# Starting the first feed-forward step's products inside the attention visits, with constant products on TensorE before them

## The chip, the cores and the metric

The kernel runs on one core of one Trainium2 chip. The metric is the device time of one execution in microseconds (us). Before the change the median of three runs is 909.93 us, from 908.02 to 910.37. Five engines work side by side and wait for each other through semaphores: TensorE (PE in the profile; its weight loads are listed as PEld), VectorE (DVE), ScalarE (ACT), GpSimd (POOL) and SyncE (SP), which here only issues DMAs. Each engine takes its instructions in the order in which the program issues them.

## What is computed

An attention over short windows, whose result is the input of a feed-forward layer. All arrays are float32; a product that needs more than the fast format of TensorE gives is made of three products of high and low parts.

```python
# attention: batch 8, heads 8, sequence 576, head_dim 64
scores = q @ k.T / 8          # masked: heads 0-3 see the last 32 keys,
attn = softmax(scores)        # heads 4-7 every 4th of the last 128 keys
x = (attn @ v) as rows of 512 # one row per token: 4608 tokens
# feed-forward: 512 -> 2048 -> 512
h = x @ w_in
g = h * erf(softplus(h))
out = g @ w_out
```

## The kernel before

**The attention in units.** The 32 head pairs (8 batches times 4 pairs) are numbered `it`; each has 9 blocks of 64 queries, and a unit is four such blocks, so there are 72 units (`NU`). A unit `n` goes through: `scores` (32 small matmuls, L214, into an `sp` bank), `mask_max` (four DVE operations, L225), `exponents` (four ACT activations, L235), `normalize` (a DVE reciprocal, L247, and a POOL product, L248), and, three units later (`LAG` = 3), `transposes` (two matmuls, L253), `turned` (a copy of the result, L257), `values` (32 small matmuls, L272), `rows` (ACT copies, L314) and `finish`, which splits a finished head pair into a high part (ACT, L319) and a low part (DVE, `part_lo`, L325). For batch 0 these parts lie in `xs[0]` to `xs[3]`, one per head pair.

**The visits.** Units 0 to 13 (`FIRST` = 14) are handled before any feed-forward work, one `first_visit(n)` each (L349 to L373): the later half of unit m = n - 3 and the early half of unit n, in a written order. On TensorE the order in a visit is transposes(m), scores(n), values(m). With nine blocks per pair and four per unit, the pairs 0, 1, 2 and 3 of batch 0 end with units 2, 4, 6 and 8, so their high parts are made in visits 5, 7, 9 and 11, and their low parts in visits 6, 8, 10 and 11. In visits 1 to 9 (`EARLY`) ACT and DVE also turn weights, which arrive as 64-bit floats, into high and low float32 parts (`prep_act`: L427, L432; `prep_dve`: L441, L445, L446, L447), and the end of each such piece lets SP load the next one (L412). The copy `turned` is ACT's in those visits, DVE's afterwards. The four pieces of `w_in` that the first two steps need come first.

**What SP does in a visit.** `load_qk(n + 2)` (L198) overwrites the buffer that scores(n) has read, so it waits for them; `load_v(n - 1)` (L202) waits for values(n - 3). SP takes its DMAs in order, so whatever stands behind such a wait starts later too.

**The steps.** The feed-forward work is cut into chunks of 512 tokens and, within these, steps of two 128-wide tiles of the 2048 features. A step `t` has two halves j = 0, 1; the main loop runs over x = 2t + j. In each half `mm1(t, j)` (L499) makes h for one tile: for each of the four 128-wide slices `cc` of the model dimension (which is a head pair) three products 128x512, twelve in all, L509, into the one PSUM bank `h`. `take` (L648, L651) copies the bank to `hc` on DVE and so frees it. In the first two steps the order in a half is: turn (transposes and the copy) of a unit, weight pieces, `mm1`, `take`, exponents, then values and scores of the next units. After both halves ACT makes softplus (L655) and erf (L658), each with a table load, DVE makes the product and its parts (`gate`: L665, L668, L669), and two steps later `mm2` (L671, L683) multiplies with `w_out` into the four `acc` banks.

**PSUM.** There are eight banks: `sp0`, `sp1`, `tx` (named `bank` in the code), `acc0` to `acc3` and `h`. During the visits, `tx` and `h` are not used; `tx` is first used by `mm1_fast`, from the fourth chunk on (L624). `plain`, an SBUF tile, is first used when the sums of weight blocks are built (`sum_whole`, L515).

Of the kernel before, what the change touches and what calls it, by code (L numbers as in the profile page):

```python
# [12 lines left out]
BF16 = mybir.dt.bfloat16  # L13
# [5 lines left out]
P = 128  # L19
# [12 lines left out]
CC = DM // P  # L32
FT = DF // P
TOK = 512
# [31 lines left out]
FREE = FIRST - LAG + 4  # L66

EARLY = 9

SAVED = 2 * (HALF + 1) + 1  # L70

# [55 lines left out]
def key_start(u, s):  # L127

    return s * STRIP + (WIN if (SPU * u) // NSTRIP != (SPU * u + s) // NSTRIP else 0)
# [7 lines left out]
def attn_moe_kernel(ctx: ExitStack, tc: tile.TileContext, qk, v, masks, eye, w_in, w_out, out):  # L137
    nc = tc.nc
# [16 lines left out]
    win_at = win.rearrange("p (a j k i c n) -> p a j k i c n", a=SPC, j=PAIR, k=2, i=2, c=2)  # L155
# [12 lines left out]
    plain = one.tile([P, 2 * TOK], F32, name="plain")  # L168
# [3 lines left out]
    bank = ps.tile([P, TOK], F32, name="tx")  # L172
# [5 lines left out]
    def place(u, p):  # L178


        if u < FREE:
            return acc[(u + 1 + 2 * p) % 4][:, p * P:(p + 1) * P]
        at = PARTS * P + (u in second) * P
        return spb[p][:, at:at + P]
# [6 lines left out]
    xs = [one.tile([P, 2, S], F32R, name=f"x{cc}") for cc in range(CC)]  # L191
# [3 lines left out]
    def load_qk(u):  # L195
        if u < NU:
            n = QW + key_start(u, SPU - 1) + KEYS
            nc.sync.dma_start(out=qkz[u % 2][:, 0:n], in_=qk[u, :, 0:n])  # L198
# [9 lines left out]
    def scores(u):  # L208
        i = u % 2
        for s in range(SPU):  # L210
            at, (p, r) = QW + key_start(u, s), divmod(s, SIDE)
            for h in range(2):
                hs = slice(h * D, (h + 1) * D)
                nc.tensor.matmul(sps[h][r * STRIP:(r + 1) * STRIP, i, p, :], qkz[i][hs, s * STRIP:(s + 1) * STRIP],  # L214
                                 qkz[i][hs, at:at + KEYS], start=True, stop=True,
                                 tile_position=(h * D, r * STRIP))

    def mask_max(u):

        pr = probs[u] = work.tile([P, 2 * PARTS, KEYS], F32, name="prob", bufs=LAG + 1)  # L220
        nmax = maxes[u] = small.tile([P, 2 * PARTS], F32, name="nmax", bufs=LAG + 1)
        for h in range(2):
            for p in range(PARTS):
                g = PARTS * h + p
                nc.vector.tensor_tensor_reduce(  # L225
                    out=pr[:, g, :], in0=sps[h][:, u % 2, p, :], in1=mask[QUADS.index(kinds(u, p))],
                    scale=-SCALE, scalar=BIG,
                    op0=ALU.add, op1=ALU.min, accum_out=nmax[:, g:g + 1],
                )
# [12 lines left out]
    def normalize(u):  # L242
        rinv = small.tile([P, 2 * PARTS], F32, name="rinv")

        if u >= FIRST:
            nc.vector.tensor_scalar(sums[u], sums[u], 1.0e-9, None, op0=ALU.add)  # L246
        nc.vector.reciprocal(out=rinv, in_=sums.pop(u))  # L247
        nc.gpsimd.tensor_tensor(probs[u], probs[u], rinv.broadcast_to([P, 2 * PARTS, KEYS]), op=ALU.mult)  # L248

    def transposes(u):  # L250
        pr = probs.pop(u)
        for h in range(2):
            nc.tensor.transpose(out=turn_place(u)[:, h * P:(h + 1) * P],  # L253
                                in_=pr[:, PARTS * h:PARTS * (h + 1), :].rearrange("p a k -> p (a k)"), identity=ident)

    def turned(u, copy):
        copy(out=pz[u in second][:, 0:2 * P], in_=turn_place(u))  # L257
# [7 lines left out]
    def values(u):  # L265
        vt, pt = vz[u % 2], pz[u in second]
        for s in range(SIDE):
            qs = slice(s * STRIP, (s + 1) * STRIP)
            for p in range(PARTS):
                ks, xp = slice(p * KEYS, (p + 1) * KEYS), place(u, p)  # L270
                for h in range(2):
                    nc.tensor.matmul(xp[h * D:(h + 1) * D, qs], vt[ks, s, h, :],  # L272
                                     pt[ks, h * P + s * STRIP:h * P + (s + 1) * STRIP], start=True, stop=True,
                                     tile_position=(p * KEYS, h * D))
# [37 lines left out]
    def rows(u):  # L312
        for to, src in rows_of(u):
            nc.scalar.copy(out=to, in_=src)  # L314
# [7 lines left out]
    def part_lo():  # L322
        while halved:
            hi, lo, src = halved.pop(0)
            nc.vector.tensor_tensor(out=lo, in0=src, in1=hi.bitcast(F32), op=ALU.subtract)  # L325
# [20 lines left out]
    def has(u):  # L346
        return 0 <= u < NU

    def first_visit(n):  # L349

        m = n - LAG
        copy = nc.scalar.copy if 1 <= n <= EARLY else nc.vector.tensor_copy
        if has(m):
            transposes(m)
        scores(n)
        load_qk(n + 2)
        if has(m):
            turned(m, copy)
        if 1 <= n <= EARLY:
            prep_act()  # L360
        if has(m):
            values(m)
        if has(n - 2):
            normalize(n - 2)
        mask_max(n)
        part_lo()
        if has(m):
            rows(m)
            finish(m)
        if m == NBLK - 1:  # L370
            part_lo()
        exponents(n)
        load_v(n - 1)  # L373
# [47 lines left out]
    def prep_act():  # L421


        calls[0] += 1
        if made:
            w, hi, lo = made.popleft()
            nc.scalar.copy(out=hi, in_=like(w, hi))  # L427
            rest.append((calls[0], w, hi, lo))
        if staged:
            i, d, hi, lo = staged.popleft()  # L430
            w = io.tile([P, TOK], F32, name="w", bufs=4)
            nc.scalar.activation(out=w, in_=d[:, :, 1].bitcast(F32), func=AF.Abs, scale=REBASE)  # L432
            begun.append((calls[0], i, d, hi, lo, w))
# [20 lines left out]
    h = ps.tile([P, TOK], F32, name="h")  # L454
# [44 lines left out]
    def mm1(t, j):  # L499
        c, ftp, _ = STEPS[t]  # L500
        hi, lo = at[c]
        ft = ftp * PAIR + j

        ccs = list(range(CC))
        if ends(t) and j == PAIR - 1:
            ccs = ccs[twice:] + ccs[:twice]
        for k, cc in enumerate(ccs):
            for i, (w, x) in enumerate(((0, hi), (0, lo), (1, hi))):
                nc.tensor.matmul(h, win_at[:, ftp, j, cc // 2, w, cc % 2, :], x[cc],  # L509
                                 start=(k == 0 and i == 0), stop=(k == CC - 1 and i == 2))  # L510

    ws = dram.tile([SPC, P, len(LEFT) * KIND], F32, name="ws")
# [133 lines left out]
    hs, ls, gs = {}, {}, {}  # L646

    def take(t, j):  # L648
        if j == 0:
            hs[t], ls[t] = (work.tile([P, PAIR, TOK], F32, name=n) for n in ("hc", "s"))  # L650
        nc.vector.tensor_copy(out=hs[t][:, j], in_=h)  # L651

    def argument(t):

# [68 lines left out]
            (nc.scalar if last and tt % 2 else nc.sync).dma_start(out=out[r:r + P, :], in_=o)  # L723

    with tc.manual_schedule():
        load_qk(0)
        nc.sync.dma_start(out=cst[:, 0:NMASK * KEYS], in_=masks)
        load_qk(1)
        nc.sync.dma_start(out=ident, in_=eye)
        for n in range(FIRST):  # L730
            if n < 3:
                load_w(n)
            first_visit(n)
            if 1 <= n <= EARLY:
                prep_dve()
# [15 lines left out]
        for x in range(2 * (NT + 2)):  # L751
            t, j = divmod(x, 2)
# [161 lines left out]
```

## Time and profile before

| | |
|---|---|
| median of the three runs | 909.93 us |
| the profiled execution | 909.24 us |
| its span, first to last instruction | 907.1 us |
| PE busy | 877.6 us, 9072 matmuls |
| DVE busy | 670.0 us |
| ACT busy | 600.5 us |
| POOL busy | 77.6 us |
| moved by DMA | 188.87 MB, 208 GB/s on average |
| visits (first scores to the transposes of unit 11) | 3.49 to 48.20 us |
| first product of h | 48.54 us |
| first product of `mm2` | 72.93 us |

A row of the timeline gives the start and the length in us, the engine, the line, the operation, the tile written and those read, shapes, and how many such instructions in a row are merged into it; in square brackets how long the engine had been idle before it, and what ended that wait. A row of the windows gives, for a stretch of time, the busy time of each engine, the DMA share and GB/s. A row of the chain of work that ended last gives start, length and what it was.

### The profile page before, as it was taken

To read this page: it belongs to the slowest core of one execution; us is meant where nothing else is said; L and a number is where in the kernel's file an instruction comes from. 1 tells how busy PE (TensorE), PEld (TensorE's weight loads), DVE (VectorE), ACT (ScalarE), POOL (GpSimd) and SP (SyncE) were. 2 spreads that over 40 slices of the span, in tenths; PEclk is the share of its full clock that TensorE was granted. 3 is DMA by queue.
4 is the path that set the end of the run, shared out by engine and by line. 5 is a ranking of instruction groups with operands and counts; after the bars stand their busy time and mean duration, and the time that the engine had idled before them with its cause. 6 is when DMAs were issued, how large, how long until landed. Compare 5 with 4: busy or idle time off the path is not lost.

```text
span 907.1 us, 22745 instructions
## 1 busy us (share of the span) xinstructions
PE 877.6 (97%) x9072; PEld 756.1 (83%) x9072; DVE 670.0 (74%) x1703; ACT 600.5 (66%) x1266; POOL 77.6 (9%) x96
## 2 busy tenths in 40 slices
PE   4699999999999999999999999999999999999998
PEld 3467777888887878888988989888988998998996
DVE  5878878876788888767866777678666866776555
ACT  7879879876678687666776676669654644545442
POOL 2312100000011100000000000001000000000000
PEclk9999999999999999999999999999999999999999
DMA  8874344433459688677668765777567546656521
GB/s 301 282 234 146 124 164 131 154 109 103 159 184 330 214 299 306 234 276 243 212 220 284 253 214 203 279 258 258 176 244 231 179 152 228 236 174 204 199 85 46
DMA packets 69449, 188.87 MB, mean 208 GB/s; under 512 B 9184, under 2 KB 17632, under 8 KB 63200
## 3 DMA queue, kind: packets, MB, share of 16 engines
q1 hardware_dynamic: 69056, 186.91, 60.4%
q8 instruction: 71, 1.16, 0.5%
q10 hardware_dynamic: 288, 0.52, 0.2%
q14 instruction: 34, 0.28, 0.1%
HBM read 153.85 MB, written 33.55 MB: 207 GB/s over the span
## 4 chain that ended last, share of the span: by engine, by line
PE 85%; DVE 7%; ACT 4%; issue 2%; DMA 2%; POOL 1%; SPq 0%; DVEq 0%; POOLq 0%; ACTq 0%
PE acc L683 40%; PE h L630 15%; PE tx L630 12%; PE h L509 11%; PE sp L272 3%; PE sp L214 2%; PE sp L253 1%; DMA dbl<-in_w_in_dram 1%; ACT prob L235 1%; DVE s L665 1%; DVE hc L651 1%; DVE w L446 1%; DVE w L447 1%; DVE ghi L668 1%; DVE win L441 0%
## 5 line engine op out<-in xcount | busy, mean ns | idle before, releaser
L683 PE MATMUL acc<-wout_hi,ghi 128*128 128x512 f32 x576 | 228.4, 396 | 0.2 <-DVE dbl L701 0.2
L683 PE MATMUL acc<-wout_lo,ghi 128*128 128x512 f32 x576 | 225.6, 392 | 0.0
L655 ACT ACTIVATE s<-hc 128x1024 f32<-128x1024 f32 x72 | 76.5, 1063 | 188.4 <-DVE hc L644 171.1
L683 PE MATMUL acc<-wout_hi,glo 128*128 128x512 f32 x576 | 158.9, 389 | 0.0
L683 PEld LDWEIGHTS acc<-wout_hi,glo 128*128 128x128 f32 x576 | 108.1, 188 | 22.7
L683 PEld LDWEIGHTS acc<-wout_hi,ghi 128*128 128x128 f32 x576 | 108.6, 188 | 20.0 <-DVE dbl L701 0.6
L683 PEld LDWEIGHTS acc<-wout_lo,ghi 128*128 128x128 f32 x576 | 108.6, 189 | 19.6
L248 POOL TENSOR_TENSOR prob<-prob,rinv 128x256 f32<-128x256 f32 x72 | 69.3, 972 | 537.6 <-DVE ssum L246 313.6
L669 DVE TENSOR_TENSOR glo<-s,ghi 128x512 fp32r<-128x512 f32 x144 | 100.0, 694 | 5.5 <-PE acc L683 0.5
L235 ACT ACTIVATE prob<-prob,nmax 128x64 f32<-128x64 f32 x288 | 96.4, 338 | 7.1 <-DVE nmax L225 6.7
L509 PE MATMUL h<-x,win 128*128 128x512 f32 x384 | 98.9, 401 | 1.2 <-DVE hc L651 1.2
L665 DVE TENSOR_TENSOR s<-hc,s 128x1024 f32<-128x1024 f32 x72 | 93.3, 1295 | 8.7 <-ACT s L658 8.6
L630 PE MATMUL h<-win 128*128 128x256 f32 x720 | 98.1, 283 | 0.0
L655 ACT ACT_TABLE_LOAD x72 | 92.4, 1283 | 1.3
L658 ACT ACT_TABLE_LOAD x72 | 92.4, 1283 | 1.3
L630 PEld LDWEIGHTS h<-win 128*128 128x128 f32 x720 | 91.6, 192 | 0.0
L509 PEld LDWEIGHTS h<-x,win 128*128 128x128 f32 x384 | 72.9, 192 | 17.8 <-DVE hc L651 2.1
L658 ACT ACTIVATE s<-s 128x1024 f32<-128x1024 f32 x72 | 76.3, 1060 | 0.8
L668 DVE CAST ghi<-s 128x512 fp32r<-128x512 f32 x144 | 68.1, 473 | 3.1 <-PE acc L683 0.6
L225 DVE CUSTOM_DVE_ANT_0 prob<-sp,cst 128x64 f32<-128x64 f32 x288 | 45.3, 219 | 30.2 <-ACT rows L314 20.5
L314 ACT COPY rows<-sp 128x128 f32<-128x128 f32 (+7 forms) x167 | 27.9, 308 | 57.0 <-PE sp L214 54.7
L640 DVE TENSOR_TENSOR hc<-h,hc 128x512 f32<-128x512 f32 x48 | 33.2, 691 | 41.2 <-PE h L630 40.9
(105 smaller groups left out, 1246.4 us busy)
## 6 DMA issues: line engine op xcount, KB each, us to landing
win<-ws SPq DMA_DIRECT2D x48, 1024.0 KB, 6.2
win<-ws SPq DMA_DIRECT2D x48, 768.0 KB, 4.5
v<-in_v_dram SPq DMA_DIRECT2D x72, 256.0 KB, 4.3
qk<-in_qk_dram SPq DMA_DIRECT2D x48, 272.0 KB, 4.1
dbl<-in_w_in_dram SPq DMA_DIRECT2D x16, 512.0 KB, 4.5
dbl<-in_w_out_dram SPq DMA_DIRECT2D x16, 512.0 KB, 3.7
ws<-x SPq DMA_DIRECT2D x32, 256.0 KB, 4.8
qk<-in_qk_dram SPq DMA_DIRECT2D x24, 288.0 KB, 4.2
```

The lines of the kernel that those rows point to most:

```text
L225: nc.vector.tensor_tensor_reduce(out=pr[:, g, :], in0=sps[h][:, u % 2, p, :], in1=mask[QUADS.index(kinds(u, p))], scale=-SCALE, scalar=BIG ...
L235: nc.scalar.activation(out=probs[u][:, j, :], in_=probs[u][:, j, :], func=AF.Exp, scale=-1.0, bias=nmax[:, j:j + 1], accum_out=sums[u][:, ...
L248: nc.gpsimd.tensor_tensor(probs[u], probs[u], rinv.broadcast_to([P, 2 * PARTS, KEYS]), op=ALU.mult)
L509: nc.tensor.matmul(h, win_at[:, ftp, j, cc // 2, w, cc % 2, :], x[cc], start=(k == 0 and i == 0), stop=(k == CC - 1 and i == 2))
L630: nc.tensor.matmul((h, bank)[b][:, half * HN:(half + 1) * HN], w[:, k, wi, c, :], x[:, xi, c, :], start=(c == 0 and n == 0), stop=(c == 1 ...
L640: nc.vector.tensor_tensor(out=a[:, 0:2], in0=x, in1=a[:, 2:3].broadcast_to([P, 2, HN]), op=ALU.add)
L655: nc.scalar.activation(out=ls[t], in_=hs[t], func=AF.Softplus)
L658: nc.scalar.activation(out=ls[t], in_=ls[t], func=AF.Erf)
L665: nc.vector.tensor_tensor(out=e, in0=hc, in1=e, op=ALU.mult)
L668: nc.vector.tensor_copy(out=ghi, in_=e[:, j])
L669: nc.vector.tensor_tensor(out=glo, in0=e[:, j], in1=ghi.bitcast(F32), op=ALU.subtract)
L683: nc.tensor.matmul(acc[tt], g[:, tt * P:(tt + 1) * P], w[:, ft, :], start=(first and w is wout_hi and g is ghi), stop=(last and g is glo))
```

## The change

Three things are added and two follow from them.

1. At the program's start GpSimd fills `idle`, the first 512 bfloat16 elements per partition of `plain`, with ones, and TensorE runs eight products `busy(8)` of these constants, 128x128 by 128x512, into the bank `h`, before anything else. Nothing reads their result.
2. In visits 0 to 6 (`AHEAD` = 7) TensorE gets more of these: six between the scores and the end of the visit in visits 0 to 2, and in visits 3 to 6 two between scores(n) and values(m) and two behind values(m). Together with the first eight these are 42.
3. In visits 7, 9 and 11 `ahead(cc)` with cc = 0, 1, 2, between scores(n) and values(m), makes the three products of slice `cc` for both halves of step 0: for j = 0 into `h`, for j = 1 into `tx`, six products a visit, 18 in all.
4. `mm1(0, 0)` and `mm1(0, 1)` are left with slice 3 alone: three products each where there were twelve.
5. `take(0, 1)` reads `tx` and not `h`. All other steps are as before.

```diff
+AHEAD = 7
...
+    idle = plain.bitcast(BF16)[:, 0:TOK]
+
+    def busy(k):
+        for _ in range(k):
+            nc.tensor.matmul(h, idle[:, 0:P], idle, start=True, stop=True)
+
+    begun_with = {}
+
+    def ahead(cc):
+        for j, to in enumerate((h, bank)):
+            begun_with.setdefault(j, to)
+            for i, (w, x) in enumerate(((0, 0), (0, 1), (1, 0))):
+                nc.tensor.matmul(to, win_at[:, 0, j, cc // 2, w, cc % 2, :], xs[cc][:, x, 0:TOK],
+                                 start=(cc == 0 and i == 0), stop=False)
+
     def first_visit(n):
...
         scores(n)
         load_qk(n + 2)
+        if n < AHEAD:
+            busy(2 if has(m) else 6)
+        elif (n - AHEAD) % 2 == 0 and (n - AHEAD) // 2 < CC - 1:
+            ahead((n - AHEAD) // 2)
         if has(m):
             turned(m, copy)
         if 1 <= n <= EARLY:
             prep_act()
         if has(m):
             values(m)
+            if n < AHEAD:
+                busy(2)
...
-        for k, cc in enumerate(ccs):
+        old = CC - 1 if t == 0 else 0
+        for k, cc in list(enumerate(ccs))[old:]:
             for i, (w, x) in enumerate(((0, hi), (0, lo), (1, hi))):
-                nc.tensor.matmul(h, win_at[:, ftp, j, cc // 2, w, cc % 2, :], x[cc],
+                nc.tensor.matmul(begun_with.get(j, h) if t == 0 else h, win_at[:, ftp, j, cc // 2, w, cc % 2, :], x[cc],
                                  start=(k == 0 and i == 0), stop=(k == CC - 1 and i == 2))
...
-        nc.vector.tensor_copy(out=hs[t][:, j], in_=h)
+        nc.vector.tensor_copy(out=hs[t][:, j], in_=begun_with[j] if t == 0 else h)
...
     with tc.manual_schedule():
+        nc.gpsimd.memset(idle, 1.0)
+        busy(8)
         load_qk(0)
```

## The prediction

> **What bounds the kernel now.** I read the page first, then the chain of work that ended last, then the timeline of the first 75 us engine by engine, then the windows of that stretch.
>
> ```profile
> span 907.1 us, 22745 instructions
> PE 877.6 (97%) x9072; PEld 756.1 (83%) x9072; DVE 670.0 (74%) x1703; ACT 600.5 (66%) x1266; POOL 77.6 (9%) x96
> ```
>
> TensorE is busy for 97% of the span, but the change neither adds nor removes a product of the result. So the place to look is where TensorE is not busy and what sets the pace there: the visits (to 48 us) and the first two steps, up to the first product of `mm2`. The chain of work holds two rows that frame this:
>
> ```profile
> 7.68 5.61 DMA dbl<-in_w_in_dram
> ...
> 73.18 2.78 PE acc L683 x12
> ```
>
> From 73.18 us on the chain is mostly TensorE at work whose order does not change. Whatever shift stands there stands at the end too, so the sum below is the shift at 73 us.
>
> Now TensorE's own timeline:
>
> ```profile
> 3.49 0.68 PE L214 MATMUL sp<-qk 64*32 64x64 f32 x32 [3.49 <-DMA qk<-in_qk_dram]
> 6.04 0.68 PE L214 MATMUL sp<-qk 64*32 64x64 f32 x32 [1.87 <-DMA qk<-in_qk_dram]
> ...
> 17.74 0.69 PE L253 MATMUL acc<-ident,prob 128*128 128x128 f32 x2 [0.72 <-POOL prob L248]
> 18.36 0.68 PE L214 MATMUL sp<-qk 64*32 64x64 f32 x32
> ...
> 39.37 0.69 PE L253 MATMUL acc<-ident,prob 128*128 128x128 f32 x2 [0.69 <-POOL prob L248]
> 39.99 0.68 PE L214 MATMUL sp<-qk 64*32 64x64 f32 x32
> 40.60 1.08 PE L272 MATMUL acc<-pT,v 64*64 64x32 f32 x32
> ...
> 48.20 0.69 PE L253 MATMUL acc<-ident,prob 128*128 128x128 f32 x2 [0.41 <-POOL prob L248]
> 48.54 5.31 PE L509 MATMUL h<-x,win 128*128 128x512 f32 x12
> 53.78 0.67 PE L272 MATMUL acc<-pT,v 64*64 64x32 f32 x32
> 54.38 0.46 PE L214 MATMUL sp<-qk 64*32 64x64 f32 x32
> 54.77 0.44 PE L253 MATMUL acc<-ident,prob 128*128 128x128 f32 x2
> 54.96 3.00 PE L509 MATMUL h<-x,win 128*128 128x512 f32 x12
> ```
>
> The same instructions take 0.69, 0.68 and 1.08 us in every visit and 0.44, 0.46 and 0.67 us from 53.78 us on; twelve products of h take 5.31 us (0.44 each) the first time and 3.00 (0.25 each) the second. TensorE runs at about 0.6 of its later speed through all visits, and speeds up only after 5.2 us without a pause. The granted clock in the windows reads 1.00 throughout, so it does not show this; the durations do.
>
> Is TensorE's slowness what sets the pace of the visits?
>
> ```profile
> 5.00:10.00 5.00, 1.37 (x64) 0.94 (x64) 1.45 (x18) 3.28 (x16) 0.44 (x2) 1.00 1.01 354
> 10.00:48.00 38.00, 26.05 (x726) 18.49 (x726) 31.50 (x138) 32.06 (x144) 13.51 (x23) 1.00 0.85 288
> 19.00:34.00 15.00, 9.65 (x278) 6.87 (x275) 14.60 (x54) 14.34 (x60) 5.45 (x9) 1.00 0.86 290
> ```
>
> Mostly not. From 5 to 10 us the DMA engines are full (1.01). From 19 to 34 us DVE is busy 14.60 of 15.00 us. TensorE matters in the short piece between, in visits 10 to 13, and in step 0, where other engines wait for it:
>
> ```profile
> 19.13 0.23 DVE L225 CUSTOM_DVE_ANT_0 prob<-sp,cst 128x64 f32<-128x64 f32 x1 [0.80 <-PE sp L214]
> ...
> 41.71 0.62 ACT L314 COPY rows<-acc 128x112 f32<-128x112 f32 x3 [1.13 <-PE acc L272]
> ...
> 43.06 0.76 DVE L325 TENSOR_TENSOR x<-rows,x 128x576 fp32r<-128x576 f32 x1 [1.64 <-ACT x L319]
> ...
> 47.54 0.61 POOL L248 TENSOR_TENSOR prob<-prob,rinv 128x256 f32<-128x256 f32 x1
> ...
> 48.93 0.42 DVE L257 COPY pT<-acc 128x256 f32<-128x256 f32 x1 [1.26 <-PE acc L253]
> ...
> 51.05 0.98 DVE L447 SCALAR_TENSOR_TENSOR w<-dbl,w 128x512 int32<-128x512 int32 x1
> ...
> 53.89 0.69 DVE L651 COPY hc<-h 128x512 f32<-128x512 f32 x1 [1.86 <-PE h L509]
> ...
> 54.48 0.50 ACT L314 COPY rows<-acc 128x64 f32<-128x64 f32 x3 [3.80 <-PE acc L272]
> ...
> 54.95 0.23 DVE L225 CUSTOM_DVE_ANT_0 prob<-sp,cst 128x64 f32<-128x64 f32 x1 [0.28 <-PE sp L214]
> ```
>
> The twelve slow products at 48.54 hold up DVE by 1.86 us and ACT by 3.80 us.
>
> **The change, part by part.** *The start.* The fill on POOL is not in the trace. Its nearest rows are the POOL product at 47.54 (256 elements in 0.61 us), so 512 elements lie between 0.1 and 1.2 us; I take 0.6. A constant product isn't in it either. It is nearest to the products of h, which have its shape: 0.44 us at the slow speed and 0.25 at the fast one. POOL has nothing else to do then. With a first DMA issue at 0.72 us, below, the eight run from 1.3 to 4.8 us. Scores(0), queued behind them, start at 4.8 where they stood at 3.49. The six behind these take 1.5 us (fast) to 2.7 us (slow), so scores(1) move from 6.04 to between 6.9 and 8.1, say by 1.5 us.
>
> ```profile
> 0.72 0.39 SPq L198 DMA_DIRECT2D qk<-in_qk_dram  x1
> ...
> 4.29 0.33 SPq L198 DMA_DIRECT2D qk<-in_qk_dram  x1
> ```
>
> Who waits for that: SP. Its third load of q and k stands behind scores(0) (issued at 4.29, now 5.6), and the weight load issued at 7.68, which is on the chain, stands behind one that waits for scores(1). That load took 5.61 us to land, because the DMA engines were full; issuing it later costs nothing as long as their queue doesn't run dry, and the full delay if it does. Between 0 and 1.5 us I take 0.5, nearer to zero because the row of 5 to 10 us shows the queue full.
>
> *The clock.* If 3.5 us of constants and what follows raise the speed within the first 8 us or so, the visits run fast from there. [...]
>
> *Visits 5 to 9.* At 17.74 the transposes and scores get faster by 0.25 and 0.22 us, and DVE's wait of 0.80 at 19.13 shrinks by that 0.47. With the 0.5 lost at the start, DVE's full stretch begins as before (+0.03). In it nothing that TensorE does counts. The constants (four a visit, 4 x 0.25 = 1.0 us, against 0.25 + 0.22 + 0.41 = 0.9 us that the speed gives back) and the products of visits 7 and 9 (6 x 0.25 = 1.5 us each) lie beside DVE's work. Were that cover gone, the two would cost about 1 us each. The products wait for weight parts and for parts of x that DVE made a visit or more before, so not at all; queued behind them on TensorE are values(m), and behind those ACT's rows, which in these visits stand behind two weight pieces of ACT's anyway.
>
> *Visits 10 to 13.* Here DVE and ACT have no weights to turn, and the chain runs through TensorE. Visit 11: transposes at 39.4, scores at 39.75, the six products from 40.15 to 41.6, values to 42.2. Before, values ended at 41.68 and ACT's rows followed at 41.71; now 0.55 later. Behind them hang ACT's split, DVE's low part (43.06), then in DVE's order the copy for unit 9, its values, faster by 0.41, ACT's rows and exponents, POOL (47.54) and the transposes at 48.20, faster by 0.25. So 0.03 + 0.55 - 0.41 - 0.25 = -0.1; DVE's copy at 48.93 moves to 48.8.
>
> *Step 0.* `mm1(0, 0)` has three products, 0.75 us: TensorE is done with it at 49.4 and with values and scores before 51. DVE turns weights until 51.05 + 0.98 = 52.03 and then copies h without the wait of 1.86 us. The wait of 0.28 at 54.95 goes too, since those scores were run long before. DVE is the late one from here; that `mm1(0, 1)` has a bank of its own, and that `mm1(1, 0)` starts early, gains nothing more, because both copies stand in DVE's order.
>
> ```profile
> 60.34 1.06 ACT L655 ACTIVATE s<-hc 128x1024 f32<-128x1024 f32 x1
> ...
> 65.05 0.42 DVE L257 COPY pT<-acc 128x256 f32<-128x256 f32 x1 [0.62 <-PE acc L253]
> ...
> 69.52 1.62 DVE L665 TENSOR_TENSOR s<-hc,s 128x1024 f32<-128x1024 f32 x1 [0.24 <-ACT s L658]
> ```
>
> The wait of 0.62 at 65.05 stays: it is POOL and TensorE following DVE's own reciprocal. The 0.24 at 69.52 goes: ACT, without its 3.80 us wait, loads its table before `hc` is there, and its softplus no longer starts at 60.34 behind a table load.
>
> The sum at 73 us: -0.1 - 1.86 - 0.28 - 0.24 = **-2.5 us**. The profiled execution took 909.24 us, so it would take 906.7; it lies 0.7 under the median of 909.93, inside the runs' spread of 2.35. On the median the forecast is **907.4 us**. A measurement of this kernel can tell about 0.3% from no change, 2.7 us; my sum lies just inside that.
>
> **The rivals.** *More gain.* If the DMA queue never runs dry, 0.5 comes back; if the products of visit 11 find cover, 0.55: -3.5 us, 906.4. For it: the full DMA row. Against: the rows of visit 11 leave no gap before values.
>
> *The speed falls back.* When the constants end with visit 6, TensorE works in visits 7 to 13 with pauses. From 10 to 48 us it was busy 26.05 of 38 us and did not speed up, so 69% in such pieces isn't enough to raise it; whether it is enough to keep it is not shown by this trace, except that after 54 us, with products of h between, it stayed. At the slow speed the six products of visit 11 take 6 x 0.44 = 2.65 us in front of values, all on the serial chain to 48.20, and step 0 still gives 2.4 back: +0.3, 910.2, no difference. [...]
>
> *Slower: the speed never rises.* Place: visits 0 to 11. Each visit 3 to 6 then has 0.69 + 0.68 + 1.08 + 4 x 0.44 = 4.2 us on TensorE, against (39.37 - 17.74) / 6 = 3.6 us a visit now: +0.6 each, 2.4 together; visits 7 and 9 add about 1 us each, visit 11 2.65, and step 0 returns 2.4: +4.7, 914.6. It decides if constants don't count as work for the clock. Against it: 4.2 us of work in 3.6 leaves no pause, and 5.2 us without a pause was enough at 48.54.
>
> *The change does nothing there.* A start that is 2 us late at the DMA would leave a gain of 1.0 us; that is inside the forecast's own case.
>
> **How the numbers follow.** Forecast case (gain 1.0 to 3.3 us) 0.64; more gain 0.12; speed falls back 0.16; never rises 0.08. Of the forecast case some 0.28 lies beyond 2.7 us: faster 0.28 + 0.12 = 0.40, slower 0.09, same 0.51. The range takes in the gain of 3.5 us and half the runs' spread (909.93 - 3.5 - 1.2 = 905.2, taken as 905.0) and the case of +0.3, 910.2, and leaves out the slow case and the tails.
>
> **What would show it.** Right: transposes, scores and values of visits 5 to 13 at 0.44, 0.46 and 0.67 us; no wait of DVE for h near 52 us; the copies for step 0 some 2 us earlier; `mm2` starting at about 70.4; the shift the same at 300 us and at the end. Wrong: the old durations in visits 7 to 13; the second weight piece landing later than 14 us; in visit 11 rows over 1 us later than 41.71; a shift at 73 us that is gone later, which would mean that a transfer or another engine, and not the order of work, sets the time after it.

## The result and the profile after

The change makes the kernel slower. Its median is 915.89 us (8 runs, 911.03 to 916.64) against 909.88 us for the kernel before (8 runs, 908.02 to 911.00): 6.0 us more. The ratio is 1.0056 with a 95% interval of 1.0040 to 1.0071: clear of no change, and about half a percent. (The ratios in this document are formed over the runs; they are not the quotients of two medians, which would be 1.0066 here.) The profiled execution took 916.24 us where that of before took 909.24.

From the page of the changed kernel, the span and the busy times:

```profile
span 914.1 us, 22830 instructions
PE 889.0 (97%) x9114; PEld 758.1 (83%) x9114; DVE 670.0 (73%) x1703; ACT 600.1 (66%) x1266; POOL 77.5 (8%) x97
```

TensorE has 42 more matmuls, the constants; the work of the other engines is the same to 0.4 us. It takes 7.0 us longer from first to last instruction. Cut into three stages, each kernel by its own TensorE timeline:

| stage of the profiled execution | before | changed |
|---|---|---|
| start to the transposes of unit 11 | 48.20 | 55.72 |
| from there to the first product of `mm2` | 24.73 | 22.99 |
| from there to the end of the span | 834.2 | 835.4 |

The visits lose 7.5 us, the first two steps give 1.7 back, and the 1.2 at the end is inside what the same stage varies by among the profiles below (833.9 to 835.4). So the question is what happened in the visits. TensorE's timeline of the changed kernel (the columns are those of the prediction's timeline):

```profile
1.29 3.46 PE L356 MATMUL h<-plain 128*128 128x512 bf16 x8 [1.29 <-POOL plain L752]
4.68 0.45 PE L216 MATMUL sp<-qk 64*32 64x64 f32 x32
5.07 1.47 PE L356 MATMUL h<-plain 128*128 128x512 bf16 x6
...
16.98 0.44 PE L255 MATMUL acc<-ident,prob 128*128 128x128 f32 x2
...
26.31 0.69 PE L255 MATMUL acc<-ident,prob 128*128 128x128 f32 x2
26.93 0.68 PE L216 MATMUL sp<-qk 64*32 64x64 f32 x32
27.53 1.65 PE L365 MATMUL h<-x,win 128*128 128x512 f32 x3
28.98 1.48 PE L365 MATMUL tx<-x,win 128*128 128x512 f32 x3
30.39 1.08 PE L274 MATMUL acc<-pT,v 64*64 64x32 f32 x32
31.40 0.61 PE L255 MATMUL acc<-ident,prob 128*128 128x128 f32 x2
...
55.72 0.69 PE L255 MATMUL acc<-ident,prob 128*128 128x128 f32 x2 [0.17 <-POOL prob L250]
```

The constants do what was forecast at the start: eight at 0.43 us, then scores at 0.45 and constants at 0.25, and the transposes of visit 5 at 16.98 where they were at 17.74 before. But from the scores of visit 6 to the values of visit 7 the lengths are the old ones or longer, and after that fast and slow stretches alternate: the next transposes take 0.61, those at 55.72 again 0.69. The speed is lost before the first early product is made, and the six products of visit 7 take from 27.53 to 30.39, 2.86 us and not 1.5; those of visits 9 and 11 take as long. Values stand behind them. Visit 7 itself begins at 26.31, 1.27 us later than before (25.04), so 6.25 of the 7.5 us arise from visit 7 on.

Who waits for values? The timeline of ACT in the changed kernel, its last weight piece in visit 7 and the next instruction, and the same a visit pair later:

```profile
27.88 0.69 ACT L457 ACTIVATE w<-dbl 128x512 f32<-128x512 f32 x1
31.50 0.56 ACT L316 COPY rows<-acc 128x128 f32<-128x128 f32 x2 [2.94 <-PE acc L274]
...
41.23 0.63 ACT L316 COPY rows<-acc 128x48 f32<-128x48 f32 x4 [2.91 <-PE acc L274]
```

ACT is free at 28.57 and idle until 31.50. All its waits for TensorE, as the waits of ACT group them, of before from 24 to 49 us and then of the changed kernel from 24 to 56 us (us in total, times, longest):

```profile
ACT rows L314 <- PE acc L272: 3.8, 4, 1.1
```

```profile
ACT rows L316 <- PE acc L274: 11.5, 5, 3.9
```

The difference, 7.7 us, is of the size of the delay. What DVE waited for in step 0 is gone, as forecast: in its waits from 48 to 76 us `hc` on TensorE falls from 1.9 us to this row of the changed kernel, whose 0.4 us stand at 74.45, in step 1:

```profile
DVE hc L677 <- PE h L535: 0.4, 1, 0.4
```

Last, the speed. The granted clock of the changed kernel is first recorded at 4.49 us, as 1.00, where the first products became fast (scores at 4.68 in 0.45 us). Up to 73 us it moves between 1.00 and 0.50 at 21.56, 31.80, 35.21, 42.04, 45.45, 48.86, 52.28, 59.10, 69.34 and 72.76, each a multiple of 3.41 us from 4.49. Windows of the changed kernel cut at such times (span, PE, PEld, DVE, ACT, POOL busy, clock, DMA share, GB/s):

```profile
7.90:11.32 3.42, 2.29 (x40) 0.83 (x38) 2.15 (x11) 2.74 (x12) 1.41 (x2) 1.00 1.02 376
...
18.14:21.56 3.42, 1.85 (x37) 0.87 (x36) 3.35 (x14) 1.99 (x8) 1.30 (x2) 1.00 0.91 299
21.56:24.97 3.41, 2.61 (x62) 1.46 (x62) 2.83 (x13) 3.41 (x16) 0.84 (x1) 0.50 0.99 329
24.97:28.38 3.41, 3.41 (x54) 1.86 (x51) 2.53 (x13) 3.34 (x14) 2.04 (x4) 0.50 0.77 231
28.38:31.80 3.42, 3.42 (x39) 2.30 (x38) 2.40 (x5) 0.48 (x3) 0.00 (x0) 0.50 0.59 209
31.80:35.21 3.41, 1.26 (x66) 0.85 (x64) 2.67 (x12) 3.41 (x15) 1.12 (x2) 1.00 0.68 206
35.21:38.62 3.41, 2.59 (x37) 1.89 (x38) 2.57 (x13) 3.11 (x15) 1.60 (x3) 0.50 0.80 244
```

After a window in which TensorE was busy for 1.85 of 3.42 us the clock is halved; it is back at 31.80, after a window filled for 3.42 us (one filled for 3.41 was not followed by it, at 28.38), and the next window, with 1.26 us of work, is followed by half speed again. The groups of visits 7, 9 and 11, from 27.53, 37.26 and 45.81 on, all run at a granted clock of 0.50. The windows before the falls at 21.56, 35.21 and 45.45 hold 1.85, 1.26 and 1.47 us of work.

### The profile page after: what moved, and what is told of

Its sections match the earlier page's. It is cut to its first block, busy times and chain, and to the rows that moved or that the text cites. A ratio compares the mean times of both kernels' runs of the same rounds, so it can differ in the third digit from the quotient of the medians.

```text
span 914.1 us, 22830 instructions
## 1 busy us (share of the span) xinstructions
PE 889.0 (97%) x9114; PEld 758.1 (83%) x9114; DVE 670.0 (73%) x1703; ACT 600.1 (66%) x1266; POOL 77.5 (8%) x97
## 4 chain that ended last, share of the span: by engine, by line
PE 86%; DVE 7%; ACT 3%; DMA 2%; issue 1%; POOL 0%; SPq 0%; DVEq 0%; POOLq 0%; ACTq 0%
PE acc L709 39%; PE h L656 15%; PE tx L656 12%; PE h L535 10%; PE sp L274 3%; PE sp L216 3%; DMA dbl<-in_w_in_dram 2%; PE sp L255 1%; ACT prob L237 1%; DVE s L691 1%; DVE hc L677 1%; PE acc L274 1%; PE h L365 1%; DVE ghi L694 0%; DVE w L472 0%
## 5 line engine op out<-in xcount | busy, mean ns | idle before, releaser
L535 PE MATMUL h<-x,win 128*128 128x512 f32 x363 | 93.4, 399 | 0.6 <-DVE hc L677 0.6
L535 PEld LDWEIGHTS h<-x,win 128*128 128x128 f32 x363 | 68.7, 192 | 15.9 <-DVE hc L677 1.1
```

The costliest lines, as they stand in the source:

```text
L535: nc.tensor.matmul(begun_with.get(j, h) if t == 0 else h, win_at[:, ftp, j, cc // 2, w, cc % 2, :], x[cc], start=(k == 0 and i == 0), stop ...
```

## The experiments

Two theories at the start. Mine: the early products cost their length because they stand in front of values, on which ACT waits (place), and they are long because the speed falls back (clock). The rival: the constants at the start delay the loads and so every visit (start). The diffs are against the changed kernel unless another is named. The time of each is the median, with its ratio to the kernel before on the same chip.

**e1_constants_only.** The constants alone; step 0 as before.

```diff
-        elif (n - AHEAD) % 2 == 0 and (n - AHEAD) // 2 < CC - 1:
-            ahead((n - AHEAD) // 2)
...
+        old = 0
```

> The 42 constants stay, the products of h go back to step 0 (twelve in each half, one bank). Clock theory (the speed falls when the constants end and half-speed products then stand in front of values on a serial chain in visits 7, 9 and 11): nothing long stands in front of values any more, the transposes of unit 11 come within 1.5 us of 48.2, 908.5 to 911. Start theory (the constants of visits 0 to 6 make loads late, and the visits after that run late): the transposes of unit 11 still at 53 us or later, 913 to 916. Place theory (six products in front of values lengthen a visit at any speed): as the clock theory, 908.5 to 911.

Measured: 911.55 us, ratio 1.0017 [1.0009, 1.0026]. The constants alone cost some 1.5 us, not 6, a little more than the 911 that the clock and place theories allowed. In its profile they are lost before visit 7, which begins 1.55 late, at 26.59; unit 11's transposes, at 49.39, are 1.19 late. TensorE's speed falls at 26.40, after the second of these windows:

```profile
12.75:16.16 3.41, 1.81 (x42) 0.95 (x38) 2.73 (x13) 2.33 (x12) 0.09 (x1) 1.00 0.87 308
...
22.99:26.40 3.41, 1.61 (x36) 0.74 (x36) 3.27 (x13) 3.41 (x17) 1.66 (x2) 1.00 0.92 298
```

**e2_products_only.** The early products and the shortened step 0, without constants.

```diff
-        if n < AHEAD:
-            busy(2 if has(m) else 6)
-        elif (n - AHEAD) % 2 == 0 and (n - AHEAD) // 2 < CC - 1:
+        if n >= AHEAD and (n - AHEAD) % 2 == 0 and (n - AHEAD) // 2 < CC - 1:
             ahead((n - AHEAD) // 2)
...
-            if n < AHEAD:
-                busy(2)
...
-        nc.gpsimd.memset(idle, 1.0)
-        busy(8)
```

> No constants; the 18 products of h stay in visits 7, 9 and 11 with their two banks. Clock theory: TensorE is at half speed through all visits, each of the three groups takes 2.9 us in front of values, the transposes of unit 11 at 53 to 56 us, 914 to 917. Start theory: without constants no load is late, 907 to 909. Place theory: 912 to 917.

Measured: 915.99 us, ratio 1.0068 [1.0054, 1.0083], and the transposes of unit 11 at 56.48. That is the changed kernel's time without a single constant: the start theory falls.

**e3_constants_throughout.** Constants, 128x256 into an unused half of `sp0`, go on through visits 7 to 13: four in front of values where no early products stand, and four behind values.

```diff
+    def filled(k):
+        for _ in range(k):
+            nc.tensor.matmul(spb[0][:, TOK // 2:TOK], idle[:, 0:P], idle[:, 0:TOK // 2], start=True, stop=True)
...
+        else:
+            filled(4)
...
+            else:
+                filled(4)
```

> The change, and in visits 7 to 13 constants too (of 128x256 into an unused half of sp0, four for each two of 128x512; in visits with products of h only behind values). Clock theory: TensorE keeps its full speed in visits 7 to 13 (values 0.67 us), the transposes of unit 11 at 48 to 50 us, 906.5 to 909.5. Start theory: as the change, 914 to 917. Place theory: three groups of 1.5 us in front of values, less 2 us in step 0, 910 to 913.

Measured: 912.60 us, ratio 1.0035 [1.0021, 1.0048]. In the profile, of its fastest run (910.91), the speed now holds until 41.15 us, visit 11, and the group of visit 7 is short:

```profile
25.82 0.96 PE L370 MATMUL h<-x,win 128*128 128x512 f32 x3
26.62 0.85 PE L370 MATMUL tx<-x,win 128*128 128x512 f32 x3
27.41 0.67 PE L274 MATMUL acc<-pT,v 64*64 64x32 f32 x32
```

1.59 us in place of 2.86. The median is 3.3 us under the changed kernel's; the two intervals overlap, so the size of this is rough. It is still slower than before, where the clock theory had said 906.5 to 909.5. How much of that is the place, how much the added constants and how much the half speed of visit 11, this run can't tell; e10 bears on it.

**e4_products_behind_values.** The same early products, behind values(m) in place of in front.

```diff
-        elif (n - AHEAD) % 2 == 0 and (n - AHEAD) // 2 < CC - 1:
-            ahead((n - AHEAD) // 2)
...
             if n < AHEAD:
                 busy(2)
+            elif (n - AHEAD) % 2 == 0 and (n - AHEAD) // 2 < CC - 1:
+                ahead((n - AHEAD) // 2)
```

> The change with the six products of visits 7, 9 and 11 behind values(m) and not in front of them. Clock theory: half-speed products now lie where TensorE waits for POOL; what they take beyond that wait (2.9 us against 0.5 to 1.8 us) still delays the next transposes, 909 to 912. Start theory: as the change, 914 to 917. Place theory: 907 to 909.

Measured: 909.59 us, ratio 0.9996 [0.9984, 1.0009]: 6.3 us off the changed kernel by the medians, 5.5 by the ratios, by moving nothing else. That is no slower than before, but no gain either: the time lies in the clock theory's range and just over the 909 of the place theory. TensorE, visits 7 and 8 (the profile is of the slowest run, 912.25):

```profile
27.89 1.08 PE L274 MATMUL acc<-pT,v 64*64 64x32 f32 x32
28.89 1.65 PE L365 MATMUL h<-x,win 128*128 128x512 f32 x3
...
31.38 0.38 PE L255 MATMUL acc<-ident,prob 128*128 128x128 f32 x2
...
32.82 0.44 PE L255 MATMUL acc<-ident,prob 128*128 128x128 f32 x2
...
64.91 0.87 PE L274 MATMUL acc<-pT,v 64*64 64x32 f32 x32 [3.90 <-DMA v<-in_v_dram]
```

and ACT:

```profile
29.00 0.57 ACT L316 COPY rows<-acc 128x128 f32<-128x128 f32 x2
```

The products of visit 7 are as slow as in the changed kernel (1.65 for three), but ACT no longer waits for values in that visit, and from 24 to 52 us its waits for values sum to 4.3 us, where they were 11.5 in the changed kernel and 3.8 before. Visit 7 is hardly shorter for it (26.64 to 31.38, 4.74 us against 5.09); visit 8 is, because ACT has gone on meanwhile: it takes 1.44 us against 4.63 (31.40 to 36.03). In the changed kernel TensorE waits in it 1.77 us for ACT's copy and then 1.20 for POOL, in e4 for neither. This is the place theory's clearest run. Its last TensorE row also shows where some of the relief goes: in step 1 values wait 3.90 us for a load of v. In SP's queue of the same kernel the load stands behind stores of x:

```profile
56.02 1.27 SPq L800 DMA_DIRECT2D x<-x  x2
...
58.23 1.65 SPq L204 DMA_DIRECT2D v<-in_v_dram  x1
```

**e10_throughout_behind** and **e12_behind_no_constants.** Place and speed crossed: e3 with the products behind values, and e4 without any constants.

The first cut is e10 against e3, the second e12 against e4.

```diff
-        elif (n - AHEAD) % 2 == 0 and (n - AHEAD) // 2 < CC - 1:
-            ahead((n - AHEAD) // 2)
...
+            elif (n - AHEAD) % 2 == 0 and (n - AHEAD) // 2 < CC - 1:
+                ahead((n - AHEAD) // 2)
```

```diff
-        if n < AHEAD:
-            busy(2 if has(m) else 6)
...
-            if n < AHEAD:
-                busy(2)
-            elif (n - AHEAD) % 2 == 0 and (n - AHEAD) // 2 < CC - 1:
+            if n >= AHEAD and (n - AHEAD) % 2 == 0 and (n - AHEAD) // 2 < CC - 1:
...
-        nc.gpsimd.memset(idle, 1.0)
-        busy(8)
```

> Constants in all visits, and the products of h of visits 7, 9 and 11 behind values: full speed and the better place together. Speed and place as two separate costs: 2 to 3 us under the run with constants throughout and products in front (912.6), 909 to 910.5, since the constants themselves cost about 1.6 us as in the run that had them alone. If the place alone matters: as the run with products behind values, 909.6, give or take 0.8. If the speed alone matters: 912 to 913.

> The 18 products behind values in visits 7, 9 and 11, no constants at all. If the constants only cost when the products lie behind values (half-speed products fit into waits for the most part): 908 to 909.5, the transposes of unit 11 at 49.5 to 51 us. If the constants help (full speed in part of the visits): 911 to 913.

Measured: 911.34 us, ratio 1.0018 [1.0004, 1.0033], and 910.58 us, ratio 1.0005 [0.9994, 1.0015]. Both are misses: e10 lies between the ranges expected for it, and so does e12.

| ratio to before | no constants | as in the change | throughout |
|---|---|---|---|
| products in front of values | 1.0068 (e2) | 1.0056 (change) | 1.0035 (e3) |
| products behind values | 1.0005 (e12) | 0.9996 (e4) | 1.0018 (e10) |

The rows differ by more than their intervals in the first two columns, and not in the third. Along the rows only the upper one falls clearly, from e2 to e3: speed is worth something where the products delay values, and no gain shows where they don't. In the third column the constants hide the place. From visit 7's transposes to unit 11's the profiles of e3, e10 and e11 (below) take 27.33, 27.64 and 27.32 us, in front or behind, where before it was 23.16. So that the place costs at half speed is shown; that it goes on costing at full speed is not.

**e6_products_twice.** The early products are made, and step 0 makes all twelve again; no constants.

```diff
-            if n < AHEAD:
-                busy(2)
...
+        old = 0
...
-        nc.gpsimd.memset(idle, 1.0)
-        busy(8)
```

> No constants; the 18 products of h are made in visits 7, 9 and 11 and then again in step 0, as in the kernel before (the early results are thrown away). It measures what the early products cost without what they save. Half-speed theory (each group of 2.9 us in front of values adds most of its length): the transposes of unit 11 at 55 to 57 us, 916.5 to 918.5. The prediction's view (DVE's work covers visits 7 and 9, visit 11 costs 2.65): 912 to 913.

Measured: 914.47 us, ratio 1.0050 [1.0037, 1.0063], unit 11's transposes at 55.82. So the early products by themselves cost about 4.5 us; the transposes stand where the half-speed theory put them, the time lies between the two forecasts. Beside e2, which has the shorter step 0 too and isn't faster, it also says that there the relief of step 0 brings nothing. The profiles show why: in e6 the groups of twelve up to `mm2` take 3.0 us each after the first, 4.46, and in e2 TensorE pauses for 3.31 us in front of values in step 1, and its next twelve take 4.67.

**e7_one_group.** Slice 0 alone, in visit 7; step 0 has nine products a half; no constants.

```diff
+        if n == AHEAD:
+            ahead(0)
...
-        old = CC - 1 if t == 0 else 0
+        old = 1 if t == 0 else 0
```

> No constants; only the six products of slice 0, in visit 7, are made early, step 0 makes nine in each half, in its two banks. Half-speed theory: visit 8 begins 2 to 3 us later than in the kernel before (27.63), step 0 gives some 0.5 back, 911.5 to 913. The prediction's view (covered by DVE's full stretch): 909 to 910.

Measured: 909.59 us, ratio 0.9996 [0.9986, 1.0005]. A miss: I had expected a loss, and the time is what the prediction's view gave. The profile is of the slowest of the twelve runs (911.34); in it the visit itself is as dear as the theory says. TensorE:

```profile
25.87 0.69 PE L255 MATMUL acc<-ident,prob 128*128 128x128 f32 x2 [0.58 <-POOL prob L250]
...
30.96 0.69 PE L255 MATMUL acc<-ident,prob 128*128 128x128 f32 x2
```

Visit 7 takes 5.09 us; before it took 27.63 - 25.04 = 2.59. That is 2.5 us. At the end of the visits 51.21 - 48.20 = 3.0 us of delay are left, of which 0.83 were there when visit 7 began. But the median shows no loss, and the shorter step 0 can hardly return more than e5, below, with all of it: 1.6. One group's cost on the median is therefore under 2 us.

**e8_first_half_even_visits.** Only the products of j = 0, into `h`, three in each of visits 8, 10 and 12, in front of values; no constants.

```diff
+        if n in (8, 10, 12):
+            ahead((n - 8) // 2)
...
+        old = CC - 1 if t == 0 and j == 0 else 0
```

> No constants; only the first half of step 0 is begun early, three products each in visits 8, 10 and 12, in front of values, where TensorE waited 1.59, 0.99 and 1.21 us before; the second half keeps its twelve, in tx. At half speed three products take 1.4 us, so they add 0 to 0.5 us a visit. The relief of the first half was seen to be worth 1.6 us at most. Half-speed theory: the transposes of unit 11 at 48 to 49.3 us, 908 to 909.5, and TensorE at full speed from about 56 us on without a fall. If place doesn't matter (any early product costs its length): 912.

Measured: 909.88 us, ratio 0.9999 [0.9991, 1.0008]. Half the products in the other visits, where TensorE had waited: no loss, so that not every early product costs its length (912), but no clear gain either.

**e5_relief_alone.** What is the relief worth by itself? The 18 products are left out altogether; no constants.

```diff
-        if n < AHEAD:
-            busy(2 if has(m) else 6)
-        elif (n - AHEAD) % 2 == 0 and (n - AHEAD) // 2 < CC - 1:
-            ahead((n - AHEAD) // 2)
...
+    begun_with.update({0: h, 1: bank})
...
-                                 start=(k == 0 and i == 0), stop=(k == CC - 1 and i == 2))
+                                 start=(k == old and i == 0), stop=(k == CC - 1 and i == 2))
```

> The kernel before, but step 0 makes only slice 3 of h (three products in each half, the second half in tx); the other 18 products are left out, nothing is added in the visits. It measures the term that the prediction gave as 1.86 + 0.28 + 0.24 us. If that term was right: 907 to 907.8. If the load of v for unit 13, which lands late in step 1, takes the place of the removed wait (load theory): 908.3 to 909.3, with DVE waiting about 2 us for scores(16) near 63 us.

Measured: 908.50 us, ratio 0.9981 [0.9971, 0.9990]: 1.6 us. I take it as the most that any place for these products can win while the rest stays. The time lies in the range of the load theory. TensorE in step 1:

```profile
61.11 0.67 PE L274 MATMUL acc<-pT,v 64*64 64x32 f32 x32 [2.91 <-DMA v<-in_v_dram]
...
62.83 4.31 PE L530 MATMUL h<-x,win 128*128 128x512 f32 x12
```

Values wait 2.91 us for v, and twelve products take 4.31 us where before, at 64.70, they took 3.02: after the pause TensorE has lost its speed as well. DVE's wait for scores is 0.7 us there, not the 2 that the load theory expected.

**e9_relief_stores_later.** e5 with the stores of x, which stand in front of that load, at x = 4.

```diff
-                if x == 0:
+                if x == 4:
```

> As the run with step 0 cut to slice 3 (18 products left out), and the two stores of x to DRAM, 512 KB each, which SP issues in step 0 ahead of the load of v for unit 13, are issued two steps later. Load theory: v lands in time, the wait near 63 us is gone, 907 to 908, about 1 us less than with the stores in place. If the load isn't what holds step 1: the same time as with the stores in place.

Measured: 908.61 us, ratio 0.9985 [0.9976, 0.9994]. No better than e5, so the load theory's forecast of 1 us failed. The wait for v is gone, and others stand in its place:

```profile
61.34 0.69 PE L255 MATMUL acc<-ident,prob 128*128 128x128 f32 x2 [3.01 <-POOL prob L250]
61.68 5.47 PE L530 MATMUL h<-x,win 128*128 128x512 f32 x12
```

The load alone was not the limit: TensorE pauses for POOL, and its next twelve take 5.47 us.

**e11_throughout_step1.** e10 with eight constants into `tx` behind `mm1` at x = 2, to keep the speed in step 1.

```diff
+                if x == 2:
+                    for _ in range(8):
+                        nc.tensor.matmul(bank, idle[:, 0:P], idle, start=True, stop=True)
```

> As the run before this one, and eight constants more in step 1, behind the products of its first half, into tx, where TensorE has paused and lost its speed in every run with step 0 cut. If the speed lost in step 1 costs: values and mm1 in 62 to 72 us at full speed, 1 to 1.5 us less than without these eight. If it costs nothing: the same time.

Measured: 912.98 us, ratio 1.0037 [1.0024, 1.0049]. A miss: no better than e10, and by the medians worse, though the intervals overlap. The speed was lost before the constants came (the `mm1` before them took 4.14) and was back when they ran (0.24 us each), and values, which follow at 65.95, stand behind them:

```profile
60.13 4.14 PE L544 MATMUL h<-x,win 128*128 128x512 f32 x12
64.12 1.90 PE L809 MATMUL tx<-plain 128*128 128x512 bf16 x8
```

**e13_relief_load_and_speed.** e9 with eight constants at the start of x = 3, in the pause.

```diff
+        nc.gpsimd.memset(idle, 1.0)
...
+            if x == 3:
+                for _ in range(8):
+                    nc.tensor.matmul(bank, idle[:, 0:P], idle, start=True, stop=True)
```

> Step 0 cut to slice 3 (18 products left out), the stores of x two steps later, and eight constants into tx at the start of the second half of step 1, where TensorE paused for 3.0 us and lost its speed. If the lost speed is what is left of the missing gain: mm1 in 61 to 65 us at 3.0 us and not 5.5, 906.5 to 907.7. If not: as with the stores moved alone, 908.6.

Measured: 907.96 us, ratio 0.9986 [0.9977, 0.9996]. The rows are what was wanted (the trace holds seven of the eight constants):

```profile
60.89 1.67 PE L781 MATMUL tx<-plain 128*128 128x512 bf16 x7 [0.16 <-issue]
...
63.93 3.02 PE L530 MATMUL h<-x,win 128*128 128x512 f32 x12
```

From the transposes of unit 11 to `mm2` it takes 71.72 - 49.78 = 21.9 us, 2.8 less than before. But the median ratio is that of e5 and e9. In the profiles of before, e5, e9 and e13, whose visits are the same instructions, unit 11's transposes stand at 48.20, 48.54, 47.39 and 49.78: one profile's visits vary by 2.4 us, and a gain of 1 us in the end time can't be read off it. Most of that arises before visit 7: from its transposes to unit 11's the same four take 23.16, 23.74, 23.29 and 23.78 us. With this 0.6 us as a ruler, the stretch took 29.41 in the changed kernel, 29.59 in e2 and 30.01 in e6 (three groups in front of values), 25.34 in e7 (one), 23.57 in e8, and between 23.46 (e12) and 25.62 (e15, below) in the four kernels with three groups behind values and no constants after visit 6.

**e15_behind_load** and **e14_behind_load_and_speed.** All products of the result again: e12 with the later stores, and e12 with the later stores and the constants at x = 3.

The second and third parts of the cut are e14's alone.

```diff
-                if x == 0:
+                if x == 4:
...
+        nc.gpsimd.memset(idle, 1.0)
...
+            if x == 3:
+                for _ in range(8):
+                    nc.tensor.matmul(bank, idle[:, 0:P], idle, start=True, stop=True)
```

> As the run before this one, without the eight constants in step 1. If the speed lost in step 1 costs: 1 to 1.5 us more than with them, 909 to 910.5. If it costs nothing: the same.

> The 18 products behind values in visits 7, 9 and 11, no constants in the visits, the stores of x two steps later, eight constants in step 1. The cost of the visits stays (transposes of unit 11 about 1 us later than 48.2), step 0 and 1 give 2 to 3 us: 907.5 to 909. If the step's gain is lost elsewhere: 910 to 911.

Measured: 908.81 us, ratio 0.9992 [0.9981, 1.0003], and 907.99 us, ratio 0.9983 [0.9973, 0.9993]. TensorE in e15, then in e14:

```profile
65.28 0.44 PE L255 MATMUL acc<-ident,prob 128*128 128x128 f32 x2 [3.01 <-POOL prob L250]
65.48 4.57 PE L531 MATMUL h<-x,win 128*128 128x512 f32 x12
```

```profile
63.61 3.03 PE L531 MATMUL h<-x,win 128*128 128x512 f32 x12
...
71.39 0.48 PE L705 MATMUL acc<-wout_hi,ghi 128*128 128x512 f32 x1
```

e14 is the one full version whose interval lies under 1, by 1.6 us in 909.55: with products behind values, the stores later and the pause of step 1 filled, step 0 and 1 take 21.7 us, from 49.71 to 71.39. The gain is 0.17%, and it is the best of several versions tried. e15 is 0.8 us above e14, a little less than the 1 to 1.5 expected if the lost speed costs; but their intervals overlap, so what the eight constants of step 1 are worth is not shown.

## Why the prediction was wrong

It said 907.4 us and got 915.89, outside its range and on the side given 0.09. By its steps:

**The start** held. The fill took 0.53 us, eight constants 0.43 each, six 0.25 each, scores(0) began at 4.68 (forecast 4.8), and the speed rose at 4.49, within the 8 us. The six behind scores(0) were fast at once, so scores(1) began at 6.47, before the range given for them (6.9 to 8.1). Visit 5 was 0.76 earlier than before (forecast +0.03), but visits that differ in nothing vary by more, and nothing of it was left when visit 7 began, 1.27 late.

**The step that failed first: "In it nothing that TensorE does counts"**, with its ground, that ACT's rows "stand behind two weight pieces of ACT's anyway". In the trace of before this cover can be measured. TensorE and ACT of before, values of visits 7 and 9 and the rows that read them:

```profile
25.04 0.69 PE L253 MATMUL acc<-ident,prob 128*128 128x128 f32 x2 [0.53 <-POOL prob L248]
...
26.62 1.08 PE L272 MATMUL acc<-pT,v 64*64 64x32 f32 x32 [0.29 <-ACT pT L257]
27.63 0.69 PE L253 MATMUL acc<-ident,prob 128*128 128x128 f32 x2
...
33.82 1.08 PE L272 MATMUL acc<-pT,v 64*64 64x32 f32 x32 [0.79 <-ACT pT L257]
```

```profile
27.85 0.56 ACT L314 COPY rows<-acc 128x128 f32<-128x128 f32 x2
...
35.16 0.62 ACT L314 COPY rows<-acc 128x48 f32<-128x48 f32 x4
```

Values end at 27.70 and 34.90, so the cover behind them is 0.15 and 0.26 us. In front of them TensorE was idle for 0.29 and 0.79. Together that is room for 0.44 and 1.05 us, for a group that even at full speed takes 1.5. The prediction itself had named the case that the cover is gone, at about 1 us for each of the two groups. ACT's row in the windows of the prediction, 14.34 busy of 15.00, should have warned: a second engine without slack, and one that waits for TensorE directly. Only DVE's was read as the limit. A delay of ACT then passes on to exponents, to POOL and to the next transposes.

**The step that failed with it: the speed holds in visits 7 to 13.** The forecast case and its better neighbour rested on it with 0.76 of the chance, and it was an estimate that no run had shown; the windows show the speed lost at 21.56, while constants were still being issued. The rival "the speed falls back" named this, with 0.16, but priced only the group of visit 11, because the first step said that visits 7 and 9 were covered: +0.3. At half speed the three groups take 2.86, 2.86 and 2.85 us. Less the room, visit 7 should be longer by 2.86 - 0.44 = 2.4 and visit 9 by 2.86 - 1.05 = 1.8; visit 11, where ACT waits for values as before, has no room, but its own transposes, scores and values were partly fast, 0.67 us in all, which leaves 2.2. Between the transposes of that visit and the next the trace shows 2.50, 1.92 and 2.09 more than before, 6.5 together. The other visits from 7 on give 0.3 back, and 1.27 were lost before visit 7, where no early product stands: 7.5. That sum is worked out from one profile; that the place is the cause at half speed is shown by e4 (5.5 to 6.3 us less), e6 and the first two columns of the table. How much the missing cover would have cost at full speed is open. By the same rows I estimate 1.5 - 0.44 - 0.88 = 0.2 us for visit 7 (0.88 is what the speed gives back in a visit, by the prediction) and nothing for visit 9, and no run tests this without further constants.

Nor did a long pause go before the fall at 21.56: of the pauses of TensorE that touch the window from 18.14 to 21.56 the longest is 0.97 us, and the clock was halved.

**Step 0: -1.86 - 0.28 - 0.24 = -2.4.** The mechanism was right: all three waits are gone from the changed kernel. But step 1 has new ones: DVE waits 1.3 us for scores at 70.14, behind a pause of TensorE of 3.29, and 0.4 for h at 74.45. So the size was wrong: alone it is 1.6 on the median (e5), and in the profiles 24.73 falls to 22.9. Not foreseen: the load of v behind the stores, and that with the shorter step 0 TensorE pauses in step 1 and its speed falls again. With both mended the stage takes 21.9 (e13) and 21.7 (e14).

**"Never rises"** had nearly the price (+4.7) but not the cause; that its 914.6 lies near the result is luck. **What would show it wrong** was apt: the old lengths stand in visits 7, 9 and 13, with fast stretches between, and the rows of visit 11 start at 49.44 and not at 41.71.

**Open.** Why the constants alone cost 1.5 us (e1) isn't settled: in its profile they are lost before visit 7, but the kernels whose visits 0 to 6 are those of before begin visit 7 anywhere from 24.10 (e9) to 26.89 (e2). Nor is the cost of one group on the median (e7) settled. The changed kernel's runs differ in their mean granted clock: 0.988 and 0.991 in the two at 911 us, 0.981 to 0.985 in the six from 914.22 to 916.64. What makes them differ is not shown.

## What to carry to other kernels

Before work is slipped into an engine's pauses, look at what is queued behind it, and measure the pause in front of that and the slack of its reader behind it: here 0.44 us together, for work of 1.5 to 2.9. Against the kernel that leaves the work out (e5, 0.9981) it cost 0.87% in front of the awaited instruction (e2) and 0.24% behind it (e12). Price such work at the slow speed as well: the six products took 2.86 us in visit 7 of the changed kernel and 1.59 in that of e3. And leave out the work altogether once (e5): here that shows that there were 1.6 us to win, not 2.4.

## What the runs showed of the hardware

The speed of TensorE fell after windows that were thinly filled, most of them without a long pause. Of the 3.41 us windows at full speed in the changed kernel, those with 1.26, 1.47, 1.61 and 1.85 us of TensorE work, in which no pause was longer than 1.84 us, were followed by half speed, and so was one with 0.66 and a pause of 3.29; those with 2.29 and more were not. In e1 1.81 held and 1.61 did not, and in e3 this one did not:

```profile
37.74:41.15 3.41, 1.97 (x73) 1.33 (x55) 2.20 (x6) 2.70 (x16) 0.83 (x2) 1.00 0.89 316
```

So 1.81 us held in e1 where 1.85 in the changed kernel and 1.97 in e3 did not: the busy time of the window alone does not tell these cases apart.

For the rise, of the windows of the changed kernel at half speed those filled for 3.42, 3.42, 3.41, 3.38 and 3.42 us were followed by full speed; those with 2.61, 2.59 and 2.85 weren't, and neither was one filled for 3.41 (24.97 to 28.38). These are nine windows of one trace, and no limit is read off them. Constants, all ones in bfloat16, were followed by a rise as products of the result were: begun at 1.29 us, by full speed at 4.49 in the changed kernel; products begun at 48.54 in the kernel before, by full speed at 53.55 (values at 53.78 in 0.67 us, where they had taken 1.08). And the clock of before reads 1.00 through visits whose transposes took 0.69 us and not 0.44; it is first recorded at 53.55, and ahead of that the lengths contradict it.
